# Linear-attention block with SwiGLU, forward and backward: an attention half, two norms and half of the gradient loads in other places

## The chip, the cores and the metric

The kernel runs on one core of a Trainium2 chip. Its time is the device time of one execution in microseconds; of several runs the median is given. The engines are called TensorE (PE, with its weight loads PEld), VectorE (DVE), ScalarE (ACT), GpSimd (POOL) and SyncE (SP, which here only issues DMAs). Each engine works through its own instructions in the order in which the program wrote them.

## The reference

The sizes are S = 2048 rows, D = 640, 32 heads of 20, F = 1728, all in bf16. The forward part is

```python
h  = x + A(layernorm(x))      # A: q, k, v = xn @ wqkv;  pq, pk = phi(q), phi(k)
                              #    kv = pk^T v;  z = sum(pk);  o = (pq kv)/(pq z + 1e-6);  A = o @ wo
h2 = h + B(layernorm(h))      # B: (silu(hn @ w1) * (hn @ w3)) @ w2
phi = lambda t: where(t > 0, t + 1, exp(t)) + 1e-6
layernorm = lambda t: (t - mean) / sqrt(var + 1e-5)
```

The kernel returns h2 and, for a given gradient of it, the gradients of x, wqkv, wo, w1, w3 and w2.

## The kernel before

The 2048 rows are cut into 16 row tiles of 128, and these into four groups of 512 rows. There is no automatic scheduling: the order of instructions on each engine is the order of the Python program, and where work of different kinds has to interleave, the program spells the order out. The stages in time are: norm of x, projections and phi (to about 75 us); joining of the attention's small matrices and the first four row tiles of its output (to about 101 us); the MLP forward with its element-wise gradients, four groups of rows (to about 327 us); gradient of w2 (to about 404 us); gradient of the second norm's input, `b_ghn`, tile by tile (to about 540 us); the gradients of the attention; the gradient of x; and last the gradients of w1 and w3.

Two places are touched.

**The step list before the MLP.** A call `run(...)` takes a list of steps written by hand. For row tile t, `f2_half(t, j)` computes column half j (320 columns) of the attention's output: five matmuls of `pqT` with `Wp` (L586) into a PSUM tile of the ring `o2` (even t) or `at` (odd t), two buffers each. For j = 0 in tiles 0 to 3, VectorE adds the PSUM tile to the row `x_sb` (L591). For j = 1 an identity matmul (L584) puts `x_sb` into the sum on TensorE and ScalarE copies the result back (L589). Either way VectorE then takes statistics of the half (L147). After the second half `part` aggregates them (L150), adds epsilon (L153), and GpSimd takes the power -1/2 (L154), which gives the factor `rs`. `f2_hn(t)` normalises the row tile into `hn[t]` on VectorE (L160) and stores it with a DMA of SyncE. `f2_ht(t)` transposes it on TensorE (L677), and ScalarE copies that into the left operand of the MLP (L678). `mlp_ghh(n)` is a chunk of five 512-column matmuls (L371) that depends on none of this and serves as filler; ScalarE copies it out (L391). `Wp` arrives by five transposing DMAs of 128 columns each; the first half of the columns needs the first three of them, the second half the last three.

`Stats` holds the statistics of a norm. Besides `norm` on VectorE it has `norm_act`, the same on ScalarE as scale times x plus bias; `bias(t)` prepares minus mean times factor on GpSimd, in two instructions (L169, L170). Before the change only tiles 10, 12 and 14 of the first norm use these (L165).

**The loop over `b_ghn`.** For each row tile t, 54 matmuls multiply the transposed gradients `ggb` with `w13a` (the first 14 of 27 row chunks) and then `w13b` (the other 13). `ggb[j]` serves two row tiles, 2j and 2j+1, and there are two buffers. `load_gg` loads chunks 0 to 13 (896 KB) at even t and chunks 14 to 26 (832 KB) at odd t, both for the next pair, both on SyncE's queue (L933), followed there by `b_load` (L989, L990) and `load_xn` (L1099). In the same loop ScalarE issues the transposing DMA of the row tile just finished, `ghT` (`b_gT`, L1037), and for t up to 10 one for `woT` or `kvN` (L1133). `ghT` is used by `b_gr` one tile later (L1057).

Of the kernel before, what the change touches and what calls it, by code (L numbers as in the profile page):

```python
# [9 lines left out]
P = 128  # L10
BF16 = mybir.dt.bfloat16
F32 = mybir.dt.float32
ALU = mybir.AluOpType
AF = mybir.ActivationFunctionType
# [4 lines left out]
S, D, H, F = 2048, 640, 32, 1728  # L19
DH = D // H  # L20
ST, DT = S // P, D // P
FT, FP = 14, 1792
# [3 lines left out]
NG = 27  # L26
# [29 lines left out]
def kernel(  # L56
# [19 lines left out]
    V, A, T, G, SY = nc.vector, nc.scalar, nc.tensor, nc.gpsimd, nc.sync  # L76
    dma, dmaT, dmaG = SY.dma_start, SY.dma_start_transpose, G.dma_start
# [26 lines left out]
    def pool(name, side="left", space=None):  # L104
        kw = dict(space=space) if space is not None else dict(side=side)
        return tc.alloc_tile_pool(name=name, bufs=1, reuse_waits="tile", **kw)

    cp = pool("cp")
# [4 lines left out]
    x_sb = x_ext[:, :, 0:D]  # L113
# [9 lines left out]
    zero = cp.tile([P, 1], F32, name="zero")  # L123
# [6 lines left out]
    class Stats:  # L130
# [13 lines left out]
        def part(self, src, t, j, mid=None):  # L144
            if j == 0:
                self.st[t] = cp.tile([P, 2, 6], F32, name="st6", bufs=4)
            V.bn_stats(out=self.st[t][:, j, :], in_=src[:, t, j * HD:(j + 1) * HD])  # L147
            if j == 0:
                return
            V.bn_aggr(out=self.mv[:, t, :], in_=self.st.pop(t)[:])  # L150
            if mid is not None:
                mid()
            V.tensor_scalar(out=self.ve[:, t:t + 1], in0=self.mv[:, t, 1:2], scalar1=EPS_LN, scalar2=None, op0=ALU.add)  # L153
            G.tensor_tensor(out=self.rs[:, t:t + 1], in0=self.ve[:, t:t + 1], in1=mhalf[:, 0:1], op=ALU.pow)  # L154
# [7 lines left out]

        def norm_act(self, out, src, t):

            A.activation(out=out, in_=src, func=AF.Identity, bias=self.nb[t][:, 1:2], scale=self.rs[:, t:t + 1])  # L165

        def bias(self, t):
            nb = self.nb[t] = cp.tile([P, 2], F32, name="nb", bufs=4)
            G.tensor_tensor(out=nb[:, 0:1], in0=self.mv[:, t, 0:1], in1=self.rs[:, t:t + 1], op=ALU.mult)  # L169
            G.tensor_tensor(out=nb[:, 1:2], in0=zero[:], in1=nb[:, 0:1], op=ALU.subtract)  # L170

    ln1, ln2 = Stats("ln1"), Stats("ln2")

# [402 lines left out]
    hn, hnT, hhT = {}, {}, {}  # L576
# [81 lines left out]
        pqs[t] = pf.tile([P, D], BF16, name="pql", bufs=4)[:]  # L658
        dma(out=pqs[t], in_=pq_v[:, t, :])

    def f2_hn(t):
        hn[t] = (pf.tile([P, D], BF16, name="hn", tag="pql", bufs=4) if 2 <= t < TPC else
                 pf.tile([P, D], BF16, name="hn", bufs=2))
        ln2.norm(hn[t][:], x_sb[:, t, :], t)
        dma(out=hn_v[:, t, :], in_=hn[t][:])

    def f2_ht(t):
# [129 lines left out]
    def kv3():  # L797
# [4 lines left out]
        (q_late, 12, lambda: (f2_wT(0), f2_wT(1))), (q_late, 13, lambda: (f2_wT(2), f2_wT(3))), (phi_rest,),  # L802
        (q_late, 14, lambda: f2_wT(4)), (load_x, 4, 8), (r_head, 5), (r_prod, 7), (r_store, 5, 6), (f2_m_out,),
        (f2_w_out,), (q_out, 8, 10), (q_out, 10, 14), (load_w2T, 8 * P, 10 * P), (mlp_ghh, 4), (q_late, 15),
        (sig_table,), (f2_half, 0, 0), (f2_half, 1, 0), (f2_half, 0, 1), (f2_half, 1, 1), (f2_hn, 0), (mlp_ghh, 5),
        (f2_half, 2, 0), (f2_hn, 1), (load_w2T, 10 * P, F), (f2_half, 2, 1), (f2_ht, 0), (f2_half, 3, 0), (f2_hn, 2),
        (f2_half, 3, 1), (f2_ht, 1), (mlp_ghh, 6), (f2_hn, 3), (f2_ht, 2), (r_red, 6), (r_inv, 6), (r_scale, 6), (r_T, 6),
        (f2_half, 4, 0), (f2_ht, 3), (mlp_ghh, 7), (f2_half, 4, 1), (r_red, 7), (r_inv, 7), (r_scale, 7), (r_T, 7),
        (r_store, 6, 8))
# [117 lines left out]

    ggb = {}

    def load_gg(j, c0, c1):  # L930
        if c0 == 0:
            ggb[j] = ba.tile([P, NG, 2 * P], BF16, name="ggb", bufs=2)
        dma(out=ggb[j][:, c0:c1, :],  # L933
            in_=gg_d[c0 * P:c1 * P, j * 2 * P:(j + 1) * 2 * P].rearrange("(c p) w -> p c w", p=P))

    def gw2_tail():
# [11 lines left out]
    for fc in range(FT - 1):  # L948
        b, i = divmod(fc, 4)
        if fc == FT - 2:  # L950
            gw2_tail()
        acc = ps.tile([P, 2, 512], F32, name="gw", bufs=4)
        for j in range(2):
            for t in range(ST):
                T.matmul(acc[:, j, 0:HD], lhsT=hb[b][:, t, i * P:(i + 1) * P], rhs=g2[:, t, j * HD:(j + 1) * HD],  # L955
                         start=(t == 0), stop=(t == ST - 1))
        ob = br.tile([P, D], BF16, name="gw2o", bufs=2)
        A.copy(out=ob[:].rearrange("p (j n) -> p j n", j=2), in_=acc[:, :, 0:HD])
        A.dma_start(out=out_6[fc * P:(fc + 1) * P, :], in_=ob[:])
        if fc == 3:  # L960
            load_hh(3)
        if fc == 5:
            load_w13()
        if fc == 8:
            load_gg(0, 0, NG)
        if fc == 11:
            load_gg(1, 0, NG)
        if fc == FT - 3:
            w13_tail()
# [17 lines left out]
    def b_load(t):  # L987
        hnb[t] = br.tile([P, D], BF16, name="hnb", bufs=3)
        dma(out=hnb[t][:], in_=hn_v[:, t, :])  # L989
        dma(out=r_sb[:, t, :], in_=r_v[:, t, :])  # L990

    def b_ghn(t):

        acc = ps.tile([P, 2, 512], F32, name="ghn", bufs=2)
        n = 0
        lo = (t % 2) * P
        for k in range(NG):
            rhs = wT[0][:, k, :] if k < FT else wT[1][:, k - FT, :]
            for j in range(2):
                T.matmul(acc[:, j, 0:HD], lhsT=ggb[t // 2][:, k, lo:lo + P], rhs=rhs[:, j * HD:(j + 1) * HD],  # L1000
                         start=(k == 0), stop=(k == NG - 1))
                n += 1
                if n % 9 == 0 and n < 54:
                    yield
        b_ln(acc, t)
# [25 lines left out]
    def by_dma(t):  # L1031
        return t < ST - 2

    def b_gT(t):
        if by_dma(t):
            ghT[t] = br.tile([P, DT, P], BF16, name="ghT", bufs=2)
            A.dma_start_transpose(out=ghT[t][:], in_=g_h[:, t, :])  # L1037
            return
        tr = ps.tile([P, DT, P], BF16, name="ght", tag="gr", bufs=2)
        for c in range(DT):  # L1040
            T.transpose(tr[:, c, :], g_h[:, t, c * P:(c + 1) * P], ident[:])
        ghT[t] = br.tile([P, DT, P], BF16, name="ghT", bufs=2)
        A.copy(out=ghT[t][:], in_=tr[:])
# [6 lines left out]
    def b_gr(t):  # L1050

        cc[t] = br.tile([P, D], F32, name="cc")
        V.tensor_tensor(out=heads(cc[t][:]), in0=heads(r_sb[:, t, :]), in1=per_head(rden[:, t, :]), op=ALU.min)
        gr[t] = ps.tile([P, 2, 512], F32, name="gr", bufs=2)
        for j in range(2):
            for c in range(DT):
                T.matmul(gr[t][:, j, 0:HD], lhsT=ghT[t][:, c, :], rhs=wT2[:, c, j * HD:(j + 1) * HD], start=(c == 0),  # L1057
                         stop=(c == DT - 1))
        pb = br.tile([P, D], F32, name="pb")
        sn = br.tile([P, H], F32, name="sn", bufs=2)  # L1060
        V.tensor_tensor(out=two(pb[:]), in0=gr[t][:, :, 0:HD], in1=two(r_sb[:, t, :]), op=ALU.mult)
        V.reduce_sum(out=sn[:], in_=heads(pb[:]), axis=AX.X)
        V.tensor_scalar(out=g_hx[:, t, D:], in0=sn[:], scalar1=-1.0, scalar2=None, op0=ALU.mult)  # L1063
        sz[t] = br.tile([P, D], F32, name="sz")
        G.tensor_tensor(out=heads(sz[t][:]), in0=heads(Zb[:]), in1=per_head(g_hx[:, t, D:]), op=ALU.mult)  # L1065

    def b_gq(t):
        V.tensor_tensor(out=two(sz[t][:]), in0=gr.pop(t)[:, :, 0:HD], in1=two(sz[t][:]), op=ALU.add)
        V.tensor_tensor(out=g_q[:, t, :], in0=sz.pop(t)[:], in1=cc.pop(t)[:], op=ALU.mult)
# [28 lines left out]
    def load_xn(a, b):  # L1098
        dma(out=xnN[:, a:b, :], in_=xn_v[:, a:b, :])  # L1099
# [12 lines left out]
    for t in range(ST):  # L1112
        g = b_ghn(t)

        def part():
            next(g, None)

        u = t - 2
        if 2 <= t <= ST - 3:
            load_gg(t // 2 + 1, *((FT, NG) if t % 2 else (0, FT)))  # L1120
        part()
        part()
        part()
        if t + 2 < ST:
            b_load(t + 2)
        if t >= 1:
            ln_rest.pop(t - 1)()
            if by_dma(t - 1):
                b_gT(t - 1)
            if t <= 2 * DT:  # L1130
                n = (t - 1) % DT
                dst, src = (woT, A_wo) if t <= DT else (kvN, kvT_d)
                A.dma_start_transpose(out=dst[:, :, n * P:(n + 1) * P], in_=src[n * P:(n + 1) * P, :])  # L1133
        part()
        if u >= 0:
            b_gr(u)
        part()
        part()
        if u >= 0:
            b_gq(u)  # L1140

        if t >= 4:
            load_xn(t - 4, t - 3)
# [152 lines left out]
    for t in range(ST):  # L1296
# [3 lines left out]
        for j in range(2):  # L1300
            for k in range(DT):
# [5 lines left out]
                               op1=ALU.mult)  # L1307
# [126 lines left out]
```

## Time and profile before

| | |
|---|---|
| median of 4 runs | 828.3 us (826.53 to 834.39) |
| the profiled execution | 826.53 us, span 824.8 us, granted TensorE clock 0.999 |
| busy in it | PE 817.0, PEld 522.5, DVE 453.9, ACT 319.1, POOL 134.1 us |
| 86 to 102 us | PE 14.93, DVE 13.93, ACT 10.32, POOL 7.25 us busy of 16 |
| 404 to 545 us | PE 141.00, DVE 94.40, ACT 28.82, POOL 17.65 us busy of 141 |

The span is the time from the first to the last instruction of the profiled execution. In the timeline a row gives the start in microseconds from the span's start, the length, the engine, the line and operation, output <- inputs with their shapes, the number of instructions merged, and in brackets the idle time before it with what ended it. "SPq" and "ACTq" are the DMA issues of SyncE and ScalarE; their length is that of the issue, not of the transfer. Matmuls are pipelined, so their lengths overlap and the distance from start to start tells their cost.

### The profile page before, as it was taken

Reading aid. Unit: us, or ns where it says so; the run is one execution under the profiler, and the core shown is the slowest. Engines: PE = TensorE matmul, PEld = TensorE weight load, DVE = VectorE, ACT = ScalarE, POOL = GpSimd, SP = SyncE. Lnnn points to the kernel's source line nnn. Section 1 sums busy time; section 2 is a strip of 40 time slices with the busy share of each in tenths; the row PEclk is TensorE's granted clock in tenths of the full one; section 3 lists DMA queues with packets and bytes.
Section 4 is the critical chain, followed back from the end, with each engine's and each line's share of the span. In section 5 each row is a group of like instructions: output and inputs, shape, how many; then the busy total and the mean of one; then the engine's idle time right before and its main releaser. Section 6 shows DMA issues by size and latency. Waiting matters only on the chain.

```text
span 824.8 us, 14217 instructions
## 1 busy us (share of the span) xinstructions
PE 817.0 (99%) x5551; PEld 522.5 (63%) x5551; DVE 453.9 (55%) x960; ACT 319.1 (39%) x609; POOL 134.1 (16%) x196
## 2 busy tenths in 40 slices
PE   8999999999999999999999999999999999999998
PEld 5677644555555555777777777777777777555554
DVE  7959897999898566300057777772681545200000
ACT  5855788655655666011121212222212334211111
POOL 2335333323323212100001111110220000000000
PEclk9999999999999999999999999999999999999999
DMA  9799999696494455999778889259995788885781
GB/s 262 206 316 216 249 240 284 201 236 171 123 223 129 148 194 167 219 250 264 216 166 182 191 216 198 62 99 190 266 216 93 164 198 181 201 198 135 160 175 38
DMA packets 318339, 157.59 MB, mean 191 GB/s; under 512 B 235456, under 2 KB 311456, under 8 KB 318272
## 3 DMA queue, kind: packets, MB, share of 16 engines
q1 hardware_dynamic: 286256, 120.65, 63.0%
q0 software_dynamic: 7376, 24.81, 9.0%
q10 hardware_dynamic: 24640, 11.23, 6.8%
q8 instruction: 43, 0.70, 0.4%
q14 instruction: 24, 0.20, 0.1%
HBM read 48.15 MB, written 51.46 MB: 121 GB/s over the span
## 4 chain that ended last, share of the span: by engine, by line
PE 94%; DVE 2%; ACT 1%; DMA 1%; SPq 1%; POOL 1%; issue 0%; DVEq 0%
PE mm L371 20%; PE job L1198 19%; PE ghn L1000 14%; PE gxn L1356 8%; PE o L766 7%; PE gw L955 7%; PE big L260 3%; PE gwo L1085 3%; PE gr L1057 3%; PE dkv L1302 3%; PE macc L402 3%; PE at L586 2%; DMA g2T<-in_grad_out_dram 1%; PE dkv L1230 1%; DVE st L147 0%; PE mm L260 0%
## 5 line engine op out<-in xcount | busy, mean ns | idle before, releaser
L1198 PE MATMUL job<-gb,hnN 128*128 128x432 bf16 (+2 forms) x656 | 117.0, 342 | 0.0
L1000 PEld LDWEIGHTS <-ggb 128*128 128x128 bf16 x864 | 84.5, 98 | 32.9
L1198 PEld LDWEIGHTS <-hnN 128*128 128x128 bf16 x656 | 63.6, 98 | 53.4
L371 PE MATMUL mm<-pqT,w 128*128 128x512 bf16 x405 | 93.7, 379 | 0.0
L371 PEld LDWEIGHTS <-w 128*128 128x128 bf16 x540 | 52.5, 98 | 63.0 <-issue 0.8
L1202 ACT CAST obs<-job 128x432 bf16<-128x432 f32 (+3 forms) x61 | 29.3, 480 | 123.1 <-PE job L1198 120.7
L766 PE MATMUL o<-w,hhT 128*128 128x320 bf16 x448 | 67.5, 299 | 0.0
L1000 PE MATMUL ghn<-w13a,ggb 128*128 128x320 bf16 x448 | 63.5, 299 | 0.0
L1000 PE MATMUL ghn<-w13b,ggb 128*128 128x320 bf16 x416 | 61.4, 299 | 0.0
L371 PE MATMUL mm<-g2T,w2T 128*128 128x512 bf16 x240 | 59.6, 379 | 0.0
L766 PEld LDWEIGHTS <-hhT 128*128 128x128 bf16 x448 | 43.8, 98 | 23.6
L955 PE MATMUL gw<-g,hb 128*128 128x320 bf16 x416 | 56.8, 299 | 0.0
L1065 POOL TENSOR_TENSOR sz<-Zb,g_h 128x640 f32<-128x640 bf16 x16 | 20.2, 1261 | 199.3 <-DVE g_h L1063 199.3
L955 PEld LDWEIGHTS <-hb 128*128 128x128 bf16 x416 | 40.6, 98 | 16.0 <-issue 0.3
L1356 PE MATMUL gxn<-wqT,gT 128*128 128x320 bf16 x320 | 48.7, 299 | 0.0
L391 ACT CAST ghh<-mm 128x512 bf16<-128x512 f32 x48 | 28.1, 586 | 46.9 <-PE mm L371 41.4
L705 ACT ACTIVATE sig<-mm 128x512 bf16<-128x512 f32 x56 | 33.5, 598 | 27.7 <-PE mm L371 25.4
L1012 ACT ACTIVATE gs<-ghn 128x640 bf16<-128x640 f32 x16 | 11.2, 703 | 79.0 <-PE ghn L1000 79.0
L371 PEld LDWEIGHTS <-w2T 128*128 128x128 bf16 x260 | 25.3, 98 | 24.7 <-issue 1.5
L260 PE MATMUL big<-wqkv,pqT 128*128 128x320 bf16 x260 | 39.4, 299 | 0.9 <-ACT pqT L256 0.6
L260 PEld LDWEIGHTS <-pqT 128*128 128x128 bf16 x320 | 30.4, 97 | 14.1 <-ACT pqT L256 2.1
L1356 PEld LDWEIGHTS <-gT 128*128 128x128 bf16 x320 | 31.3, 98 | 12.2
(201 smaller groups left out, 1282.5 us busy)
## 6 DMA issues: line engine op xcount, KB each, us to landing
hh_d<-hhT SPq DMA_DIRECT2D x24, 256.0 KB, 2.6
gg_d<-gate POOLq DMA_DIRECT2D x24, 256.0 KB, 4.0
gg_d<-ghh POOLq DMA_DIRECT2D x24, 256.0 KB, 3.5
ggb<-gg_d SPq DMA_DIRECT2D x6, 896.0 KB, 5.6
ggb<-gg_d SPq DMA_DIRECT2D x6, 832.0 KB, 7.4
x_sb<-in_A_x_dram SPq DMA_DIRECT2D x7, 640.0 KB, 6.6
out_dram<-obs ACTq DMA_DIRECT2D x39, 108.0 KB, 3.3
ggb<-gg_d SPq DMA_DIRECT2D x2, 1728.0 KB, 13.4
```

Source lines behind the costliest of these rows:

```text
L260: T.matmul(acc, lhsT=pqT[:, c, t * P:(t + 1) * P], rhs=wqkv[:, c, n0:n0 + HD], start=(c == 0), stop=(c == DT - 1))
L371: T.matmul(acc[:], lhsT=w[:, c, fc * P:(fc + 1) * P], rhs=rhs[:, c, :], start=(c == 0), stop=(c == DT - 1))
L391: A.copy(out=ghh[n // 2][:, n % 2, :], in_=acc[:])
L402: T.matmul(macc[m][j][:, 0:n], lhsT=pk_all[:, t, m * P:(m + 1) * P], rhs=x_ext[:, t, j * HD:j * HD + n], start=(t == 0), stop=(t == ST - 1))
L705: A.activation(sig[:, i, :], gp[:], AF.Sigmoid)
L766: T.matmul(o2["ps"][:, 0:HD], lhsT=hhT[c][:, fc, i * P:(i + 1) * P], rhs=w2[:, fc, j * HD:(j + 1) * HD], start=(fc == 0), stop=(fc == FT - 1))
L955: T.matmul(acc[:, j, 0:HD], lhsT=hb[b][:, t, i * P:(i + 1) * P], rhs=g2[:, t, j * HD:(j + 1) * HD], start=(t == 0), stop=(t == ST - 1))
L1000: T.matmul(acc[:, j, 0:HD], lhsT=ggb[t // 2][:, k, lo:lo + P], rhs=rhs[:, j * HD:(j + 1) * HD], start=(k == 0), stop=(k == NG - 1))
L1057: T.matmul(gr[t][:, j, 0:HD], lhsT=ghT[t][:, c, :], rhs=wT2[:, c, j * HD:(j + 1) * HD], start=(c == 0), stop=(c == DT - 1))
L1198: T.matmul(acc[:, 0:n], lhsT=lhs[:, t, m * P:(m + 1) * P], rhs=rhs(t), start=(t == 0), stop=(t == ST - 1))
L1202: A.copy(out=ob, in_=acc[:, 0:n])
L1356: T.matmul(acc[:, j, 0:HD], lhsT=g, rhs=wqT[:, k, j * HD:(j + 1) * HD], start=(k == 0), stop=(k == 14))
```

## The change

Three things are done. `f2_half(2, 0)` moves from behind the fifth filler chunk to the place after the first halves of tiles 0 and 1. The norms of tiles 1 and 2 before the MLP (`f2_hn(1)`, `f2_hn(2)`) are computed on ScalarE with a bias from GpSimd, and the bias is computed in one instruction instead of two, for the first norm's three tiles too. The second half of each gradient load leaves the head of the loop body and SyncE's queue and is issued on ScalarE's queue, behind the transposing DMA of `ghT`.

```diff
         def norm_act(self, out, src, t):
-            A.activation(out=out, in_=src, func=AF.Identity, bias=self.nb[t][:, 1:2], scale=self.rs[:, t:t + 1])
+            A.activation(out=out, in_=src, func=AF.Identity, bias=self.nb[t][:, 0:1], scale=self.rs[:, t:t + 1])

         def bias(self, t):
-            nb = self.nb[t] = cp.tile([P, 2], F32, name="nb", bufs=4)
-            G.tensor_tensor(out=nb[:, 0:1], in0=self.mv[:, t, 0:1], in1=self.rs[:, t:t + 1], op=ALU.mult)
-            G.tensor_tensor(out=nb[:, 1:2], in0=zero[:], in1=nb[:, 0:1], op=ALU.subtract)
+            nb = self.nb[t] = cp.tile([P, 1], F32, name="nb", bufs=4)
+            G.tensor_scalar(out=nb[:], in0=self.mv[:, t, 0:1], scalar1=self.rs[:, t:t + 1], scalar2=-1.0, op0=ALU.mult,
+                            op1=ALU.mult)
...
-    def f2_hn(t):
+    def f2_hn(t, on_act=False):
...
-        ln2.norm(hn[t][:], x_sb[:, t, :], t)
+        if on_act:
+            ln2.bias(t)
+            ln2.norm_act(hn[t][:], x_sb[:, t, :], t)
+        else:
+            ln2.norm(hn[t][:], x_sb[:, t, :], t)
         dma(out=hn_v[:, t, :], in_=hn[t][:])
...
-        (sig_table,), (f2_half, 0, 0), (f2_half, 1, 0), (f2_half, 0, 1), (f2_half, 1, 1), (f2_hn, 0), (mlp_ghh, 5),
-        (f2_half, 2, 0), (f2_hn, 1), (load_w2T, 10 * P, F), (f2_half, 2, 1), (f2_ht, 0), (f2_half, 3, 0), (f2_hn, 2),
+        (sig_table,), (f2_half, 0, 0), (f2_half, 1, 0), (f2_half, 2, 0), (f2_half, 0, 1), (f2_half, 1, 1), (f2_hn, 0),
+        (mlp_ghh, 5), (f2_hn, 1, True), (load_w2T, 10 * P, F), (f2_half, 2, 1), (f2_ht, 0), (f2_half, 3, 0), (f2_hn, 2, True),
         (f2_half, 3, 1), (f2_ht, 1), (mlp_ghh, 6), (f2_hn, 3), (f2_ht, 2), (r_red, 6), (r_inv, 6), (r_scale, 6), (r_T, 6),
         (f2_half, 4, 0), (f2_ht, 3), (mlp_ghh, 7), (f2_half, 4, 1), (r_red, 7), (r_inv, 7), (r_scale, 7), (r_T, 7),
...
-    def load_gg(j, c0, c1):
+    def load_gg(j, c0, c1, q=dma):
...
-        dma(out=ggb[j][:, c0:c1, :],
+        q(out=ggb[j][:, c0:c1, :],
...
-        if 2 <= t <= ST - 3:
-            load_gg(t // 2 + 1, *((FT, NG) if t % 2 else (0, FT)))
+        if 2 <= t <= ST - 3 and t % 2 == 0:
+            load_gg(t // 2 + 1, 0, FT)
...
             ln_rest.pop(t - 1)()
             if by_dma(t - 1):
                 b_gT(t - 1)
+            if 2 <= t <= ST - 3 and t % 2:
+                load_gg(t // 2 + 1, FT, NG, A.dma_start)
```

## The prediction

> **What bounds the kernel.** I read the page's busy shares first, then TensorE's own waits, then the timeline of the stretch that the edit reorders, then the gradient stage's DMA issues.
>
> ```profile
> PE 817.0 (99%) x5551; PEld 522.5 (63%) x5551; DVE 453.9 (55%) x960; ACT 319.1 (39%) x609; POOL 134.1 (16%) x196
> ```
>
> TensorE is busy 817.0 of 824.8 us at full clock. Only 7.8 us of idle time are there to win, 0.9%, so no edit that leaves the matmuls alone can bring much; what can be lost has no such ceiling. The table by stage puts 3.5 us of the idle before 86 us, 1.1 us between 86 and 102 us (where the attention halves stand), none between 102 and 545 us. So after 102 us any delay of TensorE goes straight to the end.
>
> The stretch 86 to 102 us, where the first tile group's halves, norms and transposes run (lines cut from the merged timeline: start, length, engine, line, operation, idle before it and releaser):
>
> ```profile
> 88.03 1.52 PE L586 MATMUL at<-Wp,pqT 128*128 128x320 bf16 x10
> ...
> 89.94 0.85 PE L586 MATMUL at<-Wp,pqT 128*128 128x320 bf16 x5 [0.26 <-DMA Wp<-pkx]
> ...
> 94.22 0.42 ACT L589 CAST x_sb<-at 128x320 bf16<-128x320 f32 x1 [0.91 <-PE at L586]
> ...
> 94.58 0.43 DVE L160 TENSOR_SCALAR hn<-x_sb,ln_mv,ln_rs 128x640 bf16<-128x640 bf16 x1
> 94.93 0.48 DVE L147 BATCH_NORM_STATS2 st<-x_sb 128x6 f32<-128x320 bf16 x1
> ...
> 98.03 0.55 POOL L154 TENSOR_TENSOR ln_rs<-ln_ve,mhalf 128x1 f32<-128x1 f32 x1 [1.56 <-DVE ln_ve L153]
> ...
> 98.62 0.45 DVE L160 TENSOR_SCALAR hn<-x_sb,ln_mv,ln_rs 128x640 bf16<-128x640 bf16 x1 [0.66 <-POOL ln_rs L154]
> ...
> 99.12 0.45 PE L677 MATMUL trh<-ident,hn 128*128 128x128 bf16 x5 [0.81 <-DVE hn L160]
> ```
>
> A matmul's modelled length (about 0.3 us) is not its pitch; ten 320-column matmuls take 1.36 us from start to start of the next group. So TensorE's first two first halves end at 89.39, the identity matmul takes 0.14, and the second half starts at 89.94: gap 0.41 us, for Wp's last block. The other gap is before the transpose of tile 3 (tiles count from 0): the matmuls before it end at 98.15, it starts at 99.12, gap 0.97 us, for that tile's norm. Together 1.38 us. Between, VectorE works without a pause from 93.30 to 97.95: it is the chain.
>
> **Part 1, third tile's first half moved up.** No instruction is added. TensorE runs it from 89.39 to 90.07 in place of the first gap, so 0.41 us is saved there. On VectorE its add and statistics now stand ahead of tile 0's second statistics: the statistics before them start at 90.36, so the add comes at 90.77 (pitch 0.41), its statistics at 91.28 (0.51), tile 0's second statistics at 91.69 instead of 91.29, and tile 1's variance is done at 93.44 instead of 93.04. GpSimd issues DMAs until 92.66, so tile 0's factor comes as before; its norm runs 93.37 to 93.82 and its transpose starts at 93.87. TensorE has been free since 93.61: 0.26 us of gap are new, and it is 0.15 ahead of before.
>
> **Part 2, norms of tiles 1 and 2 on ScalarE.** It removes two VectorE norms (0.35 each, 94.58 to 94.93) and adds two GpSimd bias operations and two ScalarE activations. The activation has its row, the first-stage norms at L165: 0.92 us, the next ScalarE instruction 0.81 after its start. The one-instruction bias on GpSimd is not in the trace: below, L170 (0.19); above, the power at L154 (0.55); nearest, L169 with the same operands, mean 0.33, which I take. In the first stage the same edit only shortens a GpSimd pair that runs while TensorE is busy: nothing.
>
> The added wait is what matters. Each ScalarE norm waits for statistics, power and bias, and what is queued **behind it on ScalarE** is the copy of the next second half out of PSUM (L589), for which VectorE's next statistics wait. Step by step, with starts from the rows' pitches (copy 0.43 long, statistics to aggregate 0.52, to epsilon 0.24, epsilon 0.15 long, about 0.05 to 0.09 across engines):
> - Tile 1: power 93.52, bias 94.16 to 94.49, norm 94.55. The copy of tile 2's second half, at 94.22 before, starts at 95.36 and ends at 95.79.
> - Tile 2: statistics 95.82, variance done 96.73, power 96.81, bias 97.45 to 97.78, norm 97.84 to 98.76. The copy of tile 3's second half, at 95.99 before, starts at 98.65.
> - Tile 3: statistics 99.11, variance done 100.02, power 100.10, norm on VectorE 100.70 to 101.15, transpose 101.20 against 99.12.
>
> TensorE's gaps then: 0.26, then 1.80 before tile 2's transpose (free at 97.01, norm there at 98.81), then 1.43 before tile 3's (free at 99.77). Sum 3.49 against 1.38: **+2.1 us**. What follows in TensorE's order (a filler chunk of 1.08, a half of 0.68, the first MLP matmul) keeps its distance from this transpose, so it moves whole. With the bias at 0.19 each it is +1.8, at 0.55 each +2.5. SyncE's queue hides the norms' stores: it stands in a transposed weight load from 90.82 to 98.32 anyway, and the next such load ends its issue at 103.5.
>
> A rule speaks for this part: the Trainium skill, "Perfetto Trace Analysis", section "Optimizing Scalar/DVE Operations", says that when VectorE is saturated, moving some of its work to ScalarE may pay. VectorE is indeed at 13.9 of 16.0 us here. By the rule both gaps would close, -1.4. By the rows the load moves but the latency grows: 0.92 plus a bias of 0.33 in place of 0.45, twice, ahead of a copy that the next tile needs. I take the rows.
>
> **Part 3, second half of each gradient load moved from SyncE to ScalarE's queue.** Six loads of 832 KB. At present each is issued early, right after the small loads; the move makes it late. From the timeline of that stage (SyncE's and ScalarE's DMA issues, TensorE):
>
> ```profile
> 453.73 0.39 SPq L933 DMA_DIRECT2D ggb<-gg_d  x1
> ...
> 458.08 0.43 SPq L933 DMA_DIRECT2D ggb<-gg_d  x1
> ...
> 467.36 1.22 ACTq L1037 DMA_TRANSPOSE ghT<-g_h  x1
> 468.61 1.30 ACTq L1133 DMA_TRANSPOSE kvN<-kvT_d  x1
> ...
> 474.72 1.25 PE L1000 MATMUL ghn<-w13b,ggb 128*128 128x320 bf16 x8
> ```
>
> The row at 458.08 is such a second half (453.73 a first half). After the change its issue stands between those of 467.36 and 468.61, so it starts at about 468.6, 10.5 us later. TensorE needs it at 474.72, when it turns to w13b. That leaves 6.1 us (6.1 to 6.3 in all six places). SyncE loses an issue of 0.43 that nobody waits for, and the small loads behind it are not delayed now. ScalarE gains 0.43 before the woT or kvN transpose, and its next statistics (L1012) are 2.5 us away. Even if a full queue held ScalarE 2 to 3 us, as some of its transposes take now, a transposed row issued late by that has about 3 us before its use two tiles on. Gain: none, since TensorE has no gap here.
>
> Does it land within 6.1 us? The first halves (896 KB), rather alone, land in 5.5 to 5.8 us; the second halves, in the traffic of the first halves and transposes, in 7.0 to 8.5. The stretches of one microsecond show 205, 295 and 331 GB/s from 455 to 458, after the first half issued at 453.73: 831 KB (decimal) 4.3 us after the issue, so the 852 of a second half, alone, take an estimated 4.4; the second transpose of a pair lands 0.3 later than the first, so 4.7 behind a transpose. The next first half is issued 2.6 us later on the other queue and its bytes begin 1.3 after that, so they overlap the last 0.8 us. The Trainium skill, "DMA: Bandwidth & Descriptors", "Issuing engines are not separate DMA queues", says both queues share the same 16 engines and interleave, so a new queue gives no bandwidth of its own; at half share this adds 0.8, an estimate of 5.5 and no stall. By the trace's row for the same transfer under traffic, 7.0 to 8.5, it would stall 0.9 to 2.4 us six times, 5 to 14 us. I take 5.5: that row's load stood behind the whole tail of a first half on its own queue and three small loads, which the new place does not have.
>
> **Sum.** Parts 1 and 2 together +2.1 (the 0.41 saved is inside it), part 3 nothing. Against the profiled execution (826.53, span 824.8) 828.6; against the median of the runs (828.3), which lies 1.8 above it, 830.4. I forecast on the median.
>
> **Rivals.**
> - *The gaps close as the rule has it* (-1.4: 826.9). For it: VectorE's dense row. Against: ScalarE is in order, and the copies stand behind the norms. 0.12.
> - *A gradient half lands late*, the one that ends clearly slower: at the present second-half median of 7.4 us it misses by 1.2 us, six times, 7.2; with +2.1, 837.6. It decides once landing passes 6.1 us. For it: margin only 0.6 us and DMA near full in these slices. Against: the half is moved into the emptier tile of the pair (about 100 to 125 GB/s over that tile against 255 to 270). 0.15.
> - *Edits cancel* (828.3 to 829): if the bias is short and the copies are less late than I have it, TensorE's new gaps equal the old. 0.08.
>
> The forecast itself has 0.65; its own range, by the bounds of the bias, is 830.1 to 830.8.
>
> A measurement of this kernel tells about 1% (8.3 us) from no change. Faster by that would need more idle than there is: 0.01. Slower by over 1% needs the late half at its median or worse, about two thirds of its 0.15: 0.10. The rest, 0.89, within. The range 826.0 to 837.0 takes in the closing gaps, the bias bounds, the spread of the runs (three of the four within 826.5 to 829.6), and most of the late half.
>
> **What would show it.** Right: in the profile after, TensorE waits for hn before tiles 2 and 3's transposes (some 1.8 and 1.4 us), no Wp wait at 89.9, copies at L589 start right after ScalarE norms, the first MLP matmul near 103.2 instead of 101.17, and no gap when TensorE turns to w13b. Wrong: that matmul before 101.2 (ScalarE was not the chain), or TensorE waiting for ggb near 440, 457, 475, 492, 509, 527 us (the half was late).

## The result, and the profile after

The changed kernel takes 830.84 us in the median of 43 runs (828.55 to 838.09), the kernel before 826.74 in the median of 64 (825.76 to 836.6). The ratio is 1.0043, with a 95% interval of 1.0032 to 1.0054: slower by some 3.6 us, within 1% (the two medians lie 4.1 us apart). The 828.3 us given as the time before was the median of only four runs; the larger sample lies at the profiled execution's 826.53.

The profiled execution after is 829.38 us, span 827.6 against 824.8. The page's busy line first, then TensorE's waits (total us, times, longest):

```profile
PE 817.6 (99%) x5551; PEld 523.3 (63%) x5551; DVE 452.9 (55%) x958; ACT 320.7 (39%) x611; POOL 134.6 (16%) x195
```

```profile
PE trh L681 <- ACT hn L165: 1.6, 1, 1.6
PE trh L681 <- DVE hn L160: 1.3, 1, 1.3
PE warm L441 <- DVE zero L124: 1.1, 1, 1.1
PE ghn L1004 <- DMA ggb<-gg_d: 0.9, 1, 0.9
```

TensorE has the same 5551 matmuls, and most of what was lost is idle time: 10.0 us against 7.8, of a span longer by 2.8 (the page models where matmuls end, so the other 0.6 of busy time is no added work). The first, second and fourth line are new in this size: a wait for a norm on ScalarE, a longer one for tile 3's norm on VectorE, and one for a gradient half. The wait for Wp is gone.

The stretch before the MLP, from the merged timeline after:

```profile
87.50 2.20 PE L586 MATMUL at<-Wp,pqT 128*128 128x320 bf16 x15
...
92.39 0.84 PE L586 MATMUL at<-Wp,pqT 128*128 128x320 bf16 x5
...
93.77 0.26 POOL L169 TENSOR_SCALAR nb<-ln_mv,ln_rs 128x1 f32<-128x1 f32 x1
94.06 0.92 ACT L165 ACTIVATE hn<-x_sb,nb,ln_rs 128x640 bf16<-128x640 bf16 x1 [1.02 <-POOL nb L169]
...
94.42 0.84 PE L586 MATMUL at<-Wp,pqT 128*128 128x320 bf16 x5
...
94.89 0.40 ACT L589 CAST x_sb<-at 128x320 bf16<-128x320 f32 x1
...
95.32 0.49 DVE L147 BATCH_NORM_STATS2 st<-x_sb 128x6 f32<-128x320 bf16 x1 [2.07 <-ACT x_sb L589]
...
97.28 0.92 ACT L165 ACTIVATE hn<-x_sb,nb,ln_rs 128x640 bf16<-128x640 bf16 x1 [1.40 <-POOL nb L169]
...
98.11 0.40 ACT L589 CAST x_sb<-at 128x320 bf16<-128x320 f32 x1
98.25 0.45 PE L681 MATMUL trh<-ident,hn 128*128 128x128 bf16 x5 [1.64 <-ACT hn L165]
98.54 0.49 DVE L147 BATCH_NORM_STATS2 st<-x_sb 128x6 f32<-128x320 bf16 x1 [1.36 <-ACT x_sb L589]
...
100.64 0.45 PE L681 MATMUL trh<-ident,hn 128*128 128x128 bf16 x5 [1.25 <-DVE hn L160]
...
102.69 3.62 PE L371 MATMUL mm<-pqT,w 128*128 128x512 bf16 x16
```

and its end before:

```profile
101.17 8.80 PE L371 MATMUL mm<-pqT,w 128*128 128x512 bf16 x40
```

Each copy (L589) starts 0.83 us after the ScalarE norm ahead of it. The halves that it copies are the rows of TensorE at 92.39 and 94.42, which end at 93.23 and 95.26; the copies start at 94.89 and 98.11, so they waited for ScalarE, and VectorE, which had no pause here before, now stands still for 2.07 and 1.36 us. From the first attention half (87.50) to the first MLP matmul (102.69) it is 15.19 us, against 88.03 to 101.17, 13.14, before. This length, called the stretch, is used below in place of a time in the profile, because its start moves by several tenths of a microsecond between executions with the first loads of the kernel.

The last pair of row tiles in the gradient stage, from the timelines of SyncE, ScalarE and TensorE after:

```profile
519.94 1.38 SPq L1103 DMA_DIRECT2D g<-xn_d  x3
522.36 0.59 ACTq L937 DMA_DIRECT2D ggb<-gg_d  x1
529.62 1.26 PE L1004 MATMUL ghn<-w13b,ggb 128*128 128x320 bf16 x8 [0.86 <-DMA ggb<-gg_d]
```

TensorE would have turned to w13b at 528.60; it starts at 529.62, 1.02 late. The half issued at 522.36 lands 7.2 us later. Just ahead, from 519.10 to 521.32, SyncE issues two row loads (`b_load`) and then these three xn loads in a row, the last of them 1.0 us before the half. Ahead of the pair before it stand two row loads and only one xn load, done 2.0 us before the half. The first halves, which from the second pair on overlap with the second halves, now land in 6.8 to 7.2 us (5.5 to 5.8 before); TensorE waits for none of them.

### The profile page after: what moved, and what is told of

The parts are those of the page before. It is cut to its first block, busy times and chain, and to the rows that moved or that the text cites. A ratio compares the mean times of both kernels' runs of the same rounds, so it can differ in the third digit from the quotient of the medians.

```text
span 827.6 us, 14221 instructions
## 1 busy us (share of the span) xinstructions
PE 817.6 (99%) x5551; PEld 523.3 (63%) x5551; DVE 452.9 (55%) x958; ACT 320.7 (39%) x611; POOL 134.6 (16%) x195
## 4 chain that ended last, share of the span: by engine, by line
PE 86%; DMA 1%; DVE 1%; issue 0%; ACT 0%; POOL 0%; ACTq 0%
PE mm L371 20%; PE job L1204 19%; PE ghn L1004 13%; PE gxn L1362 8%; PE o L770 7%; PE gw L959 7%; PE gwo L1089 3%; PE dkv L1308 3%; PE gr L1061 2%; PE at L586 2%; DMA ggb<-gg_d 1%; PE dkv L1236 1%; PE mm L383 0%; PE gt L945 0%; PE gkvT L1255 0%
## 6 DMA issues: line engine op xcount, KB each, us to landing
ggb<-gg_d SPq DMA_DIRECT2D x2, 1728.0 KB, 13.3
```

## The experiments

Unless it says otherwise, each starts from the kernel before.

**1 to 4: the parts apart.**

```diff
 # e1: the moved half only (norms on VectorE, loads on SyncE)
-(f2_half, 1, 0), (f2_half, 0, 1), (f2_half, 1, 1), (f2_hn, 0), (mlp_ghh, 5), (f2_half, 2, 0), (f2_hn, 1),
+(f2_half, 1, 0), (f2_half, 2, 0), (f2_half, 0, 1), (f2_half, 1, 1), (f2_hn, 0), (mlp_ghh, 5), (f2_hn, 1),
```

> Only the third tile's first half is moved; norms stay on VectorE, loads on SyncE. Theory (norms on ScalarE are what costs): the stretch from the first attention half to the first MLP matmul shrinks from 13.14 us by about 0.4 (tile 3's transpose at 98.7 against 99.12 on the old clock of the stretch, one gap of about 0.5 left before it), time -0.4 us, 826.3. Rival (the moved half itself delays VectorE's chain): the stretch grows to about 15, time +1.5 to +2 us.

Stretch 12.80, ratio 0.9996 (0.9983 to 1.0009). TensorE's only wait left in the stretch:

```profile
PE trh L677 <- DVE hn L160: 0.7, 1, 0.7
```

The moved half gains what its trace says, 0.34 us, which the ratio can't tell from nothing. It does no harm.

```diff
 # e2: the norms only, with the new bias(); f2_half(2, 0) and the loads stay
-(f2_half, 2, 0), (f2_hn, 1), ... (f2_half, 3, 0), (f2_hn, 2),
+(f2_half, 2, 0), (f2_hn, 1, True), ... (f2_half, 3, 0), (f2_hn, 2, True),
```

> Only the norms of tiles 1 and 2 go to ScalarE, with the one-instruction bias; the half and the loads stay. Theory: ScalarE's copies of tiles 2 and 3 wait behind the norms, tile 3's transpose comes about 1.7 us later than before, stretch about 14.8 us against 13.14, time +1.7 us (828.4). Rival (relieving VectorE pays, the moved half is the harm): stretch below 13, time -0.5 us or less.

Stretch 14.79, ratio 1.0035 (1.0023 to 1.0048). The stretch grows by 1.65 us, as the theory had it. TensorE's waits in this kernel name both ends of the chain:

```profile
PE trh L681 <- DVE hn L160: 1.3, 1, 1.3
PE trh L681 <- ACT hn L165: 1.1, 1, 1.1
```

The ratio is worth 2.9 us, with 1.9 as its lower end, so it is somewhat more than the stretch shows; two of its six runs have a lower clock (10 and 12 below).

```diff
 # e3: the loads only
-        if 2 <= t <= ST - 3:
-            load_gg(t // 2 + 1, *((FT, NG) if t % 2 else (0, FT)))
+        if 2 <= t <= ST - 3 and t % 2 == 0:
+            load_gg(t // 2 + 1, 0, FT)
...
                 b_gT(t - 1)
+            if 2 <= t <= ST - 3 and t % 2:
+                load_gg(t // 2 + 1, FT, NG, A.dma_start)
```

> Only the second halves of the gradient loads go to ScalarE's queue. Theory (some land late: in the profile after, one of six, by about 1 us): stretch before the MLP unchanged, TensorE waits for ggb in one or more of the six pairs, 1 to 2.5 us in all, time +1.0 to +2.5 us. Rival (the one late load is chance and the rest of the loss is in the norms): time within 0.3 us of before, no wait for ggb.

Stretch 13.02, ratio 1.0016 (1.0004 to 1.0028), +1.3 us. Two of six pairs are late, with landings of 6.5 and 7.0 us; the others land in 5.5 to 5.9. Why the earlier of the two is late was not found. From TensorE's timeline:

```profile
457.56 1.26 PE L1000 MATMUL ghn<-w13b,ggb 128*128 128x320 bf16 x8 [0.21 <-DMA ggb<-gg_d]
527.95 1.26 PE L1000 MATMUL ghn<-w13b,ggb 128*128 128x320 bf16 x8 [0.68 <-DMA ggb<-gg_d]
```

```diff
 # e4: the change with its third part undone
-        if 2 <= t <= ST - 3 and t % 2 == 0:
-            load_gg(t // 2 + 1, 0, FT)
+        if 2 <= t <= ST - 3:
+            load_gg(t // 2 + 1, *((FT, NG) if t % 2 else (0, FT)))
...
-            if 2 <= t <= ST - 3 and t % 2:
-                load_gg(t // 2 + 1, FT, NG, A.dma_start)
```

> The change without its third part: the half moved and two norms on ScalarE, loads on SyncE as before. Theory: stretch 15.2 us as in the change, no wait for ggb, time +2.0 us (828.8); the rest of the change's loss, about 1.5 to 2 us in the median, is missing here. Rival (the loss is all in the norms): as slow as the change, +3.5 to +4 us.

Stretch 15.19 again, no wait for ggb, ratio 1.0034 (1.0022 to 1.0046). With e3 it adds up to the change's 1.0043 within the intervals: most of the loss is in the norms, about a fifth (1.0043 less 1.0034) to a third (e3 alone) in the loads.

**5 and 9: is it the norm's length, or what stands behind it?**

```diff
 # e5: from e4; each ScalarE norm (with its bias) behind the next second half
-(mlp_ghh, 5), (f2_hn, 1, True), (load_w2T, 10 * P, F), (f2_half, 2, 1), (f2_ht, 0), (f2_half, 3, 0), (f2_hn, 2, True),
-(f2_half, 3, 1), (f2_ht, 1),
+(mlp_ghh, 5), (load_w2T, 10 * P, F), (f2_half, 2, 1), (f2_hn, 1, True), (f2_ht, 0), (f2_half, 3, 0),
+(f2_half, 3, 1), (f2_hn, 2, True), (f2_ht, 1),
```

> As the change without its third part, but in the step list each ScalarE norm stands behind the next second half (tile 1's norm behind tile 2's second half, tile 2's behind tile 3's), so the copy goes first on ScalarE and the norm still runs there. Theory (it is the copy queued behind the norm that costs, not the norm's length): the stretch from the first attention half to the first MLP matmul falls from 15.19 us to about 12.4 to 12.8, below the 13.14 of before; time -0.3 to -0.7 us against before. Rival (the norm's and bias's own latency costs): the stretch stays above 14 us, time +1 us or more.

A miss: ratio 1.004 (1.0028 to 1.0053). The kernel's only profile has a halved clock from 101 us on (10 and 12 below), so its stretch can't be compared; the rows below lie before that, and its ten runs at full clock have a median of 829.3 us, 2.5 above the kernel before. Its GpSimd and ScalarE rows tell why:

```profile
93.72 0.68 POOL L154 TENSOR_TENSOR ln_rs<-ln_ve,mhalf 128x1 f32<-128x1 f32 x1 [0.28 <-DVE ln_ve L153]
...
95.47 0.55 POOL L154 TENSOR_TENSOR ln_rs<-ln_ve,mhalf 128x1 f32<-128x1 f32 x1 [1.07 <-DVE ln_ve L153]
...
96.01 0.26 POOL L169 TENSOR_SCALAR nb<-ln_mv,ln_rs 128x1 f32<-128x1 f32 x1
96.31 0.92 ACT L165 ACTIVATE hn<-x_sb,nb,ln_rs 128x640 bf16<-128x640 bf16 x1 [1.87 <-POOL nb L169]
...
97.70 0.43 ACT L589 CAST x_sb<-at 128x320 bf16<-128x320 f32 x1
```

The bias moved along with the norm, and so stood on GpSimd behind the next tile's power (95.47). It came at 96.01, 7.76 us after this profile's first attention half (88.25), where in the change it came 6.27 us after it. The norm followed it, and the copy of the following tile (97.70) was held again. The same mistake, one engine further.

```diff
 # e9: from e5; the bias stays ahead, only the ScalarE norm moves
-(mlp_ghh, 5), (load_w2T, 10 * P, F), (f2_half, 2, 1), (f2_hn, 1, True), (f2_ht, 0), (f2_half, 3, 0),
-(f2_half, 3, 1), (f2_hn, 2, True), (f2_ht, 1),
+(mlp_ghh, 5), (ln2.bias, 1), (load_w2T, 10 * P, F), (f2_half, 2, 1), (f2_hn, 1, True), (f2_ht, 0), (f2_half, 3, 0),
+(ln2.bias, 2), (f2_half, 3, 1), (f2_hn, 2, True), (f2_ht, 1),
```

> As the kernel with the norms behind the copies, but the GpSimd bias stays where the change has it (ahead of the next tile's power in GpSimd's order); only the ScalarE norm stands behind the next second half. Theory (each queue must have the norm's chain ahead of what does not gate it: in the kernel before this one the bias stood behind the next tile's power on GpSimd): bias 1 at about 94.4, norm right after the copy, stretch from the first attention half to the first MLP matmul about 12.4 to 12.8 us against 15.19 of the change and 13.14 of before; time -0.3 to -0.7 us against before. Rival (norm plus bias latency itself costs on ScalarE): stretch above 14, time +1 us or more.

Stretch 12.56, ratio 0.9991 (0.9979 to 1.0002). The timeline shows the norm no shorter, but the copy in front of it:

```profile
87.47 2.20 PE L586 MATMUL at<-Wp,pqT 128*128 128x320 bf16 x15
...
93.23 0.43 ACT L589 CAST x_sb<-at 128x320 bf16<-128x320 f32 x1 [0.23 <-PE at L586]
...
93.72 0.26 POOL L169 TENSOR_SCALAR nb<-ln_mv,ln_rs 128x1 f32<-128x1 f32 x1
94.02 0.92 ACT L165 ACTIVATE hn<-x_sb,nb,ln_rs 128x640 bf16<-128x640 bf16 x1 [0.37 <-POOL nb L169]
...
100.03 8.80 PE L371 MATMUL mm<-pqT,w 128*128 128x512 bf16 x39
```

and e4, for comparison:

```profile
88.28 2.20 PE L586 MATMUL at<-Wp,pqT 128*128 128x320 bf16 x15
...
103.47 2.75 PE L371 MATMUL mm<-pqT,w 128*128 128x512 bf16 x12
```

With the same instructions on the same engines as e4, the stretch is 2.63 us shorter. So the cost was the order, not the 0.92 us of the norm. Against e1, which leaves these norms on VectorE (12.80), the hand-over in the right order gains 0.24 us of the stretch, which the ratios can't tell from nothing.

**6 and 7: why the gradient half is late.**

```diff
 # e6: from e3; the second half one row tile earlier, still behind the transposing DMA on ScalarE's queue
-            if 2 <= t <= ST - 3 and t % 2:
+            if 2 <= t <= ST - 3 and t % 2 == 0:
                 load_gg(t // 2 + 1, FT, NG, A.dma_start)
```

> Only the loads change: second halves on ScalarE's queue behind the transposing DMA, but one row tile earlier, at even t. Theory (the loads cost because they are issued late, 6.2 us before use): no wait for ggb in any of six pairs, time within 0.3 us of before. Rival (a large load on ScalarE's queue behind transposes is slow in itself or holds up ScalarE): waits for ggb or for ghT remain, time +1 us or more.

No wait for ggb, ratio 0.999 (0.9979 to 1.0), landings 6.0 us in the median. So ScalarE's queue does no harm here; the lateness was in the row tile chosen.

```diff
 # e7: from e3; the last three xn loads left to the load after the loop
-        if t >= 4:
+        if 4 <= t < ST - 3:
             load_xn(t - 4, t - 3)
...
-    load_xn(ST - 4, ST)
+    load_xn(ST - 7, ST)
```

> As the loads-only kernel, but the small xn loads of the last three row tiles are left to one load after the loop, so that SyncE does not issue three of them just ahead of the last second half. Theory (the last pair is late because those loads share the engines with it): its landing falls from 7.0 us to about 5.7 and its wait of 0.7 us is gone, time about 0.7 us less than loads-only (+0.3 to +0.6 against before, if the later load of seven xn tiles is hidden). Rival (the last pair is late for another reason): landing stays near 7 us and the wait stays.

The last half lands in 5.4 us instead of 7.0 (e3) or 7.2 (the change and its second profile), no wait for ggb is left in the profile, and the ratio is 0.9999 (0.9985 to 1.0013). The rows of the change and of e7:

```profile
ggb<-gg_d ACTq DMA_DIRECT2D x1, 832.0 KB, 7.2
```

```profile
ggb<-gg_d ACTq DMA_DIRECT2D x1, 832.0 KB, 5.4
```

The three small loads were what made the last pair late. SyncE issues them together because the last two row tiles have neither a row load nor a gradient load that would stand between them.

**8 and 11: what the stretch can give.**

```diff
 # e8: from e1; tile 4's second half ahead of tile 3's transpose
-(f2_half, 4, 0), (f2_ht, 3), (mlp_ghh, 7), (f2_half, 4, 1),
+(f2_half, 4, 0), (f2_half, 4, 1), (f2_ht, 3), (mlp_ghh, 7),
```

> The moved half alone, norms on VectorE and loads on SyncE, and the fifth tile's second half placed ahead of the fourth tile's transpose, the filler chunk behind it. Theory: both gaps of the stretch are then covered, the stretch falls from 13.14 us to about 12.0, time -1.0 us (0.13%) against before. Rival (the transpose's copy then holds the first MLP matmul, or the delay comes back in VectorE): stretch above 12.6, time within 0.4 us of before.

Stretch 12.11, no wait for a norm, ratio 0.9987 (0.9972 to 1.0001), so just not clear of no gain.

> The two versions that came out at or under before, together: moved half with the fifth tile's second half ahead of the fourth transpose (0.9987), and second gradient halves on ScalarE's queue one row tile earlier (0.999). Theory: the two touch different stages, stretch 12.1 us, no wait for ggb, ratio 0.998, about 825.2. Rival (the second ratio is noise, since TensorE has no gap in that stage to win): ratio 0.9987 as without it.

This one is e8 with the loads of e6. Stretch 12.12, no wait for a norm, Wp or ggb, ratio 0.9978 (0.997 to 0.9985), median 825.52 us: faster than both kernels, if only by 0.2% against the kernel before. Its interval overlaps that of e8, and its profiled span (823.6) is no shorter than e8's (823.4), so that the earlier loads add anything is not shown.

**10 and 12: the rest of the loss.** Of the change's 44 runs (the median above leaves one out), 22 show a granted clock of 0.998 or less, with a median of 831.49 us; the other 22 have 830.20. Of 138 runs of the kernel before that shared chips with the experiments, 7 do. The share by kernel: e5 12 of 22, e2 2 of 6, e3 2 of 8, e4 1 of 5, against e1 0 of 13, e6 0 of 22, e7 1 of 22, e8 2 of 22, e9 1 of 13, e11 0 of 18. (The "3 of 84" in the expectation below was 3 of 97 by then.) The pauses are not all of it: e3, whose longest wait in the stretch is the 0.7 us that the kernel before has too, still has 2 of 8. The only profile that caught it is e5's (835.87 us, its slowest run), in stretches of one microsecond (length, busy time of PE, PEld, DVE, ACT, POOL, PEclk, which is the granted clock, then DMA share, GB/s):

```profile
99.00:100.00 1.00, 0.00 (x0) 0.00 (x0) 0.09 (x1) 0.00 (x0) 0.80 (x2) 1.00 0.89 301
100.00:101.00 1.00, 0.02 (x1) 0.02 (x2) 0.00 (x0) 1.00 (x2) 0.00 (x0) 1.00 1.14 232
101.00:102.00 1.00, 1.00 (x7) 0.79 (x8) 0.00 (x0) 1.00 (x3) 0.00 (x0) 0.50 1.08 230
...
110.00:111.00 1.00, 1.00 (x3) 0.30 (x2) 0.90 (x5) 0.00 (x0) 0.00 (x0) 0.50 1.16 364
111.00:112.00 1.00, 1.00 (x5) 0.44 (x4) 0.97 (x4) 0.43 (x1) 0.88 (x2) 0.88 0.88 273
```

and TensorE's rows in the same profile:

```profile
97.28 0.45 PE L681 MATMUL trh<-ident,hn 128*128 128x128 bf16 x5 [1.28 <-ACT hn L165]
97.57 1.24 PE L371 MATMUL mm<-g2T,w2T 128*128 128x512 bf16 x5
100.98 0.72 PE L681 MATMUL trh<-ident,hn 128*128 128x128 bf16 x5 [2.17 <-ACT hn L165]
```

The five matmuls at 97.57 take 1.08 us from start to start, so TensorE pauses from 98.65 to 100.98, and when it comes back its clock is at half, for ten microseconds. That fits the mean: 0.994 over 834 us is 5.0 us of clock lost, half of ten. By the same sum a mean of 0.998 is an estimated 1.7 us lost, near the 1.3 us between the two medians of the change. The next kernel is the change with the pauses filled:

```diff
 # e10: from the change, in f2_ht
         tr = ps.tile([P, DT, P], BF16, name="trh", tag="mm", bufs=4)
+        for n in range({2: 24, 3: 18}.get(t, 0)):
+            T.transpose(tr[:, n % DT, :], ident[:], ident[:])
```

> The change, with matmuls that compute nothing (24 and 18 transposes of the identity, about 1.3 and 1.0 us) put on TensorE ahead of the transposes of tiles 2 and 3, into the same PSUM tile, which the real transposes overwrite. They fit into the waits of 1.8 and 1.4 us. Theory (in the runs of the change with a granted clock of 0.998 or less, about half of them, the two long pauses of TensorE let the clock gate halve the clock for some us): stretch unchanged at 15.2 us, runs with a clock of 0.998 or less become rare, as in before (3 of 84), median down by 0.5 to 1 us against the change, to about 829.9 to 830.3. Rival (the lower clock has nothing to do with the pauses): still about half of the runs at 0.998 or less, median 830.8.

All 6 runs have a clock of 0.999 or 1.0 and the stretch is 15.18, as expected; were it still half of the runs, six in a row would come in about 1 of 64 cases. But the time went the other way: 834.33 us, ratio 1.0088 (1.0072 to 1.0104). The page's groups give the reason:

```profile
L1006 PE MATMUL ghn<-w13b,ggb 128*128 128x320 bf16 x416 | 61.5, 299 | 3.6 <-DMA ggb<-gg_d 3.6
```

Here all six second halves are late, with landings of 6.6 to 7.3 us. Nothing in the edit touches them. e9, e10 and e11 ran on one chip, which no other experiment used, but the chip alone does not explain it: e11's second halves, on ScalarE's queue and one row tile earlier, land there in 5.9 us in the median, and e6's, at the same place on another chip, in 6.0. In e10 other loads of the same gradients are longer as well: the first halves take 7.9 us (7.0 in the change), and the two large loads before the loop 14.2 (13.3). The change itself was then profiled again.

> The change itself, unaltered, profiled a second time. In the kernel with the filled pauses all six second halves were late (3.6 us of waits, landing 6.6 to 7.3 us) against one of six in the first profile of the change. Theory (the window of 6.2 us is so close to the transfer's length that chips and executions fall on either side of it): the number of late pairs, their landings and the time differ from the first profile's one late pair, anywhere from 829 to 834 us, with the wait for ggb following the landing. Rival (the added matmuls made the loads late): one late pair, the last, as in the first profile, and a median of 830.8 us within 0.4 on any chip.

Ratio 1.0045 (1.0031 to 1.0059), stretch 15.19, and one late pair of six, the last, by 0.85 us of wait: as in its first profile. The theory, that the number of late pairs would move, missed; the rival had the late pair right, though not the median (830.03, where it allowed 830.4 at the least). This was the chip of e1 to e4, so whether e10's six late halves come from its chip together with this place for the loads, or from the kernel with the added matmuls, stays open: the change was not run on e10's chip.

## Why the prediction was right or wrong

**The whole.** 830.4 was forecast and 830.84 measured, but part of that is luck: the sum was put on a median of four runs that lay 1.6 us above the kernel's own. From the 826.74 of the larger sample the same sum gives 828.8, 2.0 short. The difference was forecast as +2.1 us, against +3.6 by the ratio.

**Part 1** was right: no Wp wait, and alone the moved half takes 0.34 us off (e1). On its own it costs nothing.

**Part 2** was right in mechanism and size. Predicted for the stretch +2.1 us, measured +2.05; on the clock of the stretch before, the first MLP matmul comes at 103.22, where 103.2 was forecast. The waits were forecast at 1.80 and 1.43 us; by the distances of the starts (TensorE free at 96.46 and 99.22) they are 1.79 and 1.42. The bias took 0.26, not 0.33, but the power ahead of tile 1's took 0.68 instead of 0.55, and the two cancel. That the queue behind the norm is the cause, which was argued, is shown by e9 against e4. The rule that a saturated VectorE may hand work to ScalarE was not wrong: e9 follows it and is at or below the kernel before. It says nothing of order, and order decided. It was also not needed: e8 closes both gaps with the norms left on VectorE.

**Part 3** was the term mis-sized: 0 was forecast, about +1 us measured (1.02 in the profile; 1.3 by the ratio of e3). Five halves land in 5.6 to 5.9 us, close to the 5.5 of the estimate. The step that failed is the claim that small loads ahead of the half are something "which the new place does not have", made for all six places alike. For the last pair SyncE, with no other load between them, issues three xn loads at once, the last 1.0 us ahead of the half, and the half took 7.2. They were to be seen in the profile before:

```profile
518.23 1.38 SPq L1099 DMA_DIRECT2D g<-xn_d  x3
```

The rival's row for the transfer under traffic (7.0 and up) was the right price for this pair and the wrong one for the five others. With only 0.3 to 0.6 us to spare, the others are late too in some executions: one more in e3, all in e10.

**What was missing.** Runs with a clock of 0.998 or less are half of the change's and are 1.3 us slower in the median. No term stood for that: the pauses were priced at their length alone. That the pauses cause it is not shown: it rests on the shares by kernel, one profile (e5, whose pauses are longer) and six runs of e10, and no run of the change itself was profiled with it. Stretch and last pair together are 3.1 us; the 22 runs at full clock are 830.20, 3.5 above the median before, and the remaining 0.4 us is not located.

That the time stays within 1% was given 0.89 and came true, but it says little for the argument: all that it needed was that there was little idle time to win and that no term of the loss came near 8 us.

## What to carry to other kernels

When work moves to an engine that has time to spare, price it by what stands behind it in that engine's order, and by every helper instruction's place on its own engine: the same two norms cost 2 us in front of a copy and nothing measurable behind it. A load that is moved closer to its use needs its landing time compared with the time left until its use, case by case, the last iteration too, where other queues have run ahead. And where TensorE hardly paused, a new pause may cost more than its length; one profile here shows that.

## What the runs showed of the hardware

A pause of TensorE of 2.3 us (98.65 to 100.98 in e5, after one of 1.4 us and 1.4 us of work) was followed by ten microseconds at half clock, which is 5 us of work not done. The Trainium skill, "TensorE: Matmul & The Clock Gate", section "Part 1: The HAM clock gate (the "warmup" mystery)", puts the drop to half after at least one idle window of about 3.4 us, with the window running free. By that, no pause of these kernels would cost more than its own length. Here the longest unbroken pause before the drop was shorter than such a window, and the clock fell; the measurement decides, and that the pauses on both sides of the short work count together is a guess. A window that runs free would fit with the change's being hit in half of its runs; that too is not tested.
